# Two chained feed-forward layers behind windowed attention: the first batch's value rows loaded for all heads at once

## The chip, the cores and the metric

The kernel runs on one core of a Trainium2 chip. The metric is device time in microseconds (us) of one execution; the median of three executions of the kernel before is 607.07 us (607.02 to 609.26).

## The reference

Attention over 2 batches, 8 heads, 768 positions and 64 columns a head, then two feed-forward layers over the 1536 tokens. Each position sees the 31 keys within 15 places of its own, and 24 block summaries: the maximum of the keys and the mean of the values over blocks of 32.

```python
k_sum = k.reshape(B, H, nb, block, D).max(axis=3)
v_sum = v.reshape(B, H, nb, block, D).mean(axis=3)
scores_l = scale * q @ k.T            # kept where |i - j| < 16, else -1e9
scores_s = scale * q @ k_sum.T + log(block)
a = softmax(concat(scores_l, scores_s))
x = a @ concat(v, v_sum)              # 1536 x 512 after the heads are joined
x = (silu(x @ w_gate) * (x @ w_val)) @ w_out     # d_ff 1536
h = x @ w_in2
out = (h * tanh(softplus(h))) @ w_out2           # d_ff 2048
```

## The kernel before

**Work.** Attention goes in 24 units: batch `b`, third of the sequence `tb` (256 positions, four query tiles of 64), pair of heads `p` (units 0 to 3 are `b` 0, `tb` 0). A unit has scores (L468, `scores`), a softmax (DVE L504, L534 to L544, ACT L521), a transposition (L558) and the product with the values (L573, `values`), whose result is kept as a high and a low part, `xh` and `xl`, of reduced-precision products. The first feed-forward layer is cut into 42 items (chunk `c` of the hidden columns by token group `g`); `hidden` (L822) makes gate and value, `out_half` (L873) and `out_products` (L921) multiply by `w_out`. Later items go through `block_unit` (L1179), which saves products by sums and differences of quarters. The second layer is items 42 to 89. Feed-forward products are run as three products of high and low parts.

**Weights.** They come as 64-bit words, 512 KB to a load, through `words32` (loads `t0`, `t1`, ...): one of `NRAW` = 3 buffers `raw`, an ACT operation (L725), two or three on DVE (L732, L741, L752), then a copy (ACT, L279) and a difference (DVE, L293) give the high and low part in `wsl`. The first are `t0` (gate, chunk 0), `t1` (value), `t2` (out), `t3` to `t5` for chunk 1 and `t6` to `t8` for chunk 2. A load into `raw` can start when the words that lay there have been read.

**First batch.** `do_k` loads the transposed keys of a pair (`k0` to `k3`, into `pacc`), takes block maxima (DVE, L321) and copies all twelve overlapping key windows of 96 to `kext` on GpSimd (POOL in the profile), though units 0 to 3 read the loaded keys directly. `means_first` loads the 768 value rows as six tiles of 128 (`m0` to `m5`, 256 KB each) into scratch buffers, makes the block means of all heads in PSUM bank 0 with six fp32 products (L346; each is two instructions in the trace), and four copies, on ACT and DVE in turn (L279, L285), spread them into the value buffer `vext`. Apart from this each unit loads its own value rows (`load_v`, loads `w0`, `w1`, ...): windows of 96 rows for four query tiles by the 128 columns of its pair, 192 KB in pieces of 512 bytes. One `vext` serves all thirds and both batches.

**Order.** All operations are first collected with their dependencies and a latest time, worked back from wanted times. `Program.order` then plays them through with a model of costs and writes one fixed order for each engine and for the DMA queue of SyncE (SP in the profile). Where TensorE has nothing in that model, it puts in products on a constant tile `warm` (L266), which nobody reads. The first loads have a list of their own, `FIRST_LOADS`. Before the first operation of TensorE it puts `FILL_FIRST` = 4 of the L266 products.

Of the kernel before, what the change touches and what calls it, by code (L numbers as in the profile page):

```python
# [17 lines left out]
P = 128  # L18
# [4 lines left out]
TQ = 64  # L23
# [3 lines left out]
CCOLS = 3 * KC + P + KC + NB - P // BLOCK  # L27
# [29 lines left out]

JOIN, PAIRED = 6, 12
# [6 lines left out]
VX = ("ACT", "DVE", "ACT", "DVE")  # L65
# [3 lines left out]
def constants():  # L69
# [9 lines left out]
    out[np.arange(P), 3 * KC + P + KC - P // BLOCK + np.arange(P) // BLOCK] = 1.0 / BLOCK  # L79
# [18 lines left out]
class Program:  # L98
# [3 lines left out]
    def __init__(self):  # L102
        self.ops = []

        self.fill, self.fill_to = None, 0
        self.last_write = {}
        self.readers = {}

    def add(self, eng, cost, fn, r=(), w=(), want=None, rel=0.0):
# [15 lines left out]
        self.ops.append(dict(eng=eng, cost=cost, fn=fn, deps=sorted(deps), want=want, rel=rel))  # L125

    def order(self):
# [6 lines left out]
        dma_latency, hop = 3200.0, 250.0  # L134
        own = dict(PE=0.0, ACT=120.0, DVE=120.0, POOL=120.0, SP=0.0)
        late = [0.0] * len(ops)
        for n in range(len(ops) - 1, -1, -1):
            o = ops[n]
            t = min((late[s] for s in after[n]), default=1e9) - o["cost"] - hop
            if o["eng"] == "SP":  # L140
                t -= dma_latency
            late[n] = t if o["want"] is None else min(t, o["want"])
        left = [len(o["deps"]) for o in ops]
        ready = [o["rel"] for o in ops]
        free = dict.fromkeys(own, 0.0)
        dma_free = 1000.0
        waiting = {e: [n for n, o in enumerate(ops) if o["eng"] == e and not left[n]] for e in own}
        done = []
        while any(waiting.values()):
            best = None  # L150
            for e, c in waiting.items():
                if c:
                    t = max(free[e], min(ready[n] for n in c))
                    if e == "SP":
                        t = max(t, dma_free - 1500.0)
# [6 lines left out]
            if e == "PE" and self.fill:  # L162
                gap = t - free["PE"]
                done += [self.fill] * (FILL_FIRST if not free["PE"] else max(0, int(FILL * gap / 430.0)))
                if n == self.fill_to:
                    self.fill = None
            done.append(o["fn"])
            if e == "SP":
                free[e] = t + 450.0
                dma_free = max(dma_free, t) + o["cost"]  # L170
                end = dma_free + dma_latency
            else:
                free[e] = end = t + o["cost"]
            for s in after[n]:
# [4 lines left out]
        return done  # L179
# [10 lines left out]
def c_pool(n):  # L190
    return 100 + 2.35 * n
# [7 lines left out]
def tile_kernel(  # L199
# [25 lines left out]
    mean = cst[:, 3 * KC + P :]  # L225
    xh = many(NGRP, [P, KD, GRP], F32R, "xh")
# [1085 lines left out]
```

## Time and profile before

| | us |
|---|---|
| median of 3 runs | 607.07 |
| the profiled execution, its own time | 605.46 |
| its span, first to last instruction | 603.5 |
| TensorE busy in the span | 594.7 (99%) |
| VectorE busy | 443.8 (74%) |
| ScalarE busy | 332.3 (55%) |
| GpSimd busy | 25.0 (4%) |

The profiled execution lies 1.96 us outside its span and 1.61 us under the median. PE is TensorE, PEld its weight load, DVE VectorE, ACT ScalarE, POOL GpSimd, SPq the queue that issues DMAs. The L266 products count as busy time, so a busy TensorE isn't always one that does needed work. The mean granted clock of TensorE was 0.999 of full speed.

### The profile page before, as it was taken

What the parts mean: (1) busy time and instruction counts of PE and PEld (TensorE: products, weight loads), DVE (VectorE), ACT (ScalarE), POOL (GpSimd) and SP (SyncE); (2) the same over time, 40 slices, a digit from 0 to 9 for tenths busy, and PEclk for the clock granted to TensorE, in tenths of its full rate; (3) what the DMA queues carried; (4) which work ended last, traced back from release to release, by engine and by line L of the source; (5) the groups of instructions that cost most, each with busy time, mean ns of one, the idle gap of its engine ahead of it and who ended that gap; (6) DMA issues with size and microseconds to landing.
All of it is one profiled execution on the core that took longest, in us unless ns stands there. A gap on an engine that the chain in (4) does not pass through costs nothing.

```text
span 603.5 us, 10209 instructions
## 1 busy us (share of the span) xinstructions
PE 594.7 (99%) x3858; PEld 507.2 (84%) x3858; DVE 443.8 (74%) x1005; ACT 332.3 (55%) x764; POOL 25.0 (4%) x37
## 2 busy tenths in 40 slices
PE   8999999999999999999999999999999999999997
PEld 6688899988988889988889778988888889988875
DVE  6898689687498958858948999996574476972333
ACT  4787689655464635634525666766553465643230
POOL 3213220000000000000000000000000000000000
PEclk9999999999999999999999999999999999999999
DMA  9988566004100321302401301332130040300103
GB/s 321 303 240 220 128 197 201 29 6 153 52 1 0 141 70 45 133 33 71 141 0 33 108 2 35 105 140 84 56 107 34 1 139 1 106 0 1 70 1 139
DMA packets 34768, 55.02 MB, mean 91 GB/s; under 512 B 8712, under 2 KB 23176, under 8 KB 34720
## 3 DMA queue, kind: packets, MB, share of 16 engines
q1 hardware_dynamic: 34720, 54.38, 28.4%
q8 instruction: 30, 0.49, 0.3%
q14 instruction: 18, 0.15, 0.1%
HBM read 50.98 MB, written 3.15 MB: 90 GB/s over the span
## 4 chain that ended last, share of the span: by engine, by line
PE 93%; DVE 3%; DMA 2%; ACT 1%; issue 0%; SPq 0%; DVEq 0%
PE bank L1179 38%; PE bank L921 34%; PE bank L822 11%; PE bank L873 3%; PE bank L468 2%; PE bank L573 2%; PE bank L558 2%; DMA raw<-in_w_gate_dram 1%; DVE pacc L952 1%; PE bank L346 1%; DMA att<-in_qt_dram 1%; DVE pacc L293 1%; PE bank L266 0%; DVE xl L1079 0%; PE bank L382 0%
## 5 line engine op out<-in xcount | busy, mean ns | idle before, releaser
L1179 PE MATMUL bank<-xh,wsl 128*128 128x256 f32 (+1 forms) x512 | 142.5, 336 | 0.0
L921 PE MATMUL bank<-wsl,gt 128*128 128x512 f32 x576 | 139.1, 390 | 0.2 <-DVE pacc L952 0.2
L921 PEld LDWEIGHTS bank<-wsl,gt 128*128 128x128 f32 x576 | 106.0, 188 | 20.8 <-ACT gt L279 0.6
L1179 PEld LDWEIGHTS bank<-xh,wsl 128*128 128x128 f32 x512 | 92.0, 189 | 11.2
L293 DVE TENSOR_TENSOR tmps<-tmps,bank 128x256 f32<-128x256 f32 (+1 forms) x93 | 51.3, 551 | 66.9 <-PE bank L1179 56.5
L921 PE MATMUL bank<-gt,wsl 128*128 128x512 f32 x360 | 92.3, 392 | 1.0 <-DVE pacc L952 0.6
L1179 PE MATMUL bank<-att_late,wsl 128*128 128x512 f32 (+1 forms) x352 | 86.8, 370 | 0.0
L1179 PE MATMUL bank<-xl,wsl 128*128 128x256 f32 (+1 forms) x256 | 85.9, 336 | 0.0
L279 ACT ACTIVATE wsl<-cva 128x512 fp32r<-128x512 f32 (+1 forms) x100 | 59.1, 594 | 41.7 <-DVE cva L752 10.1
L921 PEld LDWEIGHTS bank<-gt,wsl 128*128 128x128 f32 x360 | 65.7, 188 | 14.9 <-DVE pacc L952 2.0
L822 PE MATMUL bank<-xh,wsl 128*128 128x256 f32 (+1 forms) x288 | 77.9, 328 | 0.3 <-DVE tmps L1131 0.3
L1179 PEld LDWEIGHTS bank<-att_late,wsl 128*128 128x128 f32 x352 | 64.8, 188 | 12.1 <-ACT tmps L279 0.2
L293 DVE TENSOR_TENSOR wsl<-cva,wsl 128x512 fp32r<-128x512 f32 (+1 forms) x100 | 63.8, 644 | 11.4 <-ACT wsl L279 9.9
L279 ACT ACTIVATE tmps<-bank 128x512 f32<-128x512 f32 (+1 forms) x80 | 39.1, 491 | 56.4 <-PE bank L1179 49.8
L293 DVE TENSOR_TENSOR gt<-tmps,gt 128x512 fp32r<-128x512 f32 (+1 forms) x77 | 49.6, 644 | 25.7 <-PE bank L921 13.9
L279 ACT ACTIVATE gt<-tmps 128x512 fp32r<-128x512 f32 (+1 forms) x76 | 44.9, 591 | 29.7 <-PE bank L921 21.8
L1201 ACT ACTIVATE tmps<-tmps 128x512 f32<-128x512 f32 (+1 forms) x66 | 34.5, 522 | 48.3 <-DVE tmps L293 48.1
L822 PEld LDWEIGHTS bank<-xh,wsl 128*128 128x128 f32 x288 | 51.6, 189 | 6.8 <-issue 1.8
L1179 PEld LDWEIGHTS bank<-xl,wsl 128*128 128x128 f32 x256 | 48.4, 189 | 6.3
L741 DVE SCALAR_TENSOR_TENSOR cva<-cvs,cva 128x512 uint32<-128x512 uint32 x68 | 46.7, 691 | 1.2
L725 ACT ACTIVATE cvs<-raw 128x512 f32<-128x512 f32 x68 | 45.0, 667 | 3.5 <-DMA raw<-in_w_val_dram 1.7
L822 PE MATMUL bank<-xl,wsl 128*128 128x256 f32 (+1 forms) x144 | 45.8, 318 | 0.0
(104 smaller groups left out, 721.1 us busy)
## 6 DMA issues: line engine op xcount, KB each, us to landing
raw<-in_w_out_dram SPq DMA_DIRECT2D x28, 512.0 KB, 3.7
raw<-in_w_in_dram SPq DMA_DIRECT2D x16, 512.0 KB, 3.6
raw<-in_w_gate_dram SPq DMA_DIRECT2D x12, 512.0 KB, 3.5
raw<-in_w_val_dram SPq DMA_DIRECT2D x12, 512.0 KB
att<-in_vt_dram SPq DMA_DIRECT2D x24, 192.0 KB, 5.4
att<-in_qt_dram SPq DMA_DIRECT2D x24, 128.0 KB, 4.5
out_dram<-pacc SPq DMA_DIRECT2D x8, 256.0 KB, 2.1
pacc<-in_kt_dram SPq DMA_DIRECT2D x4, 400.0 KB, 5.0
```

Source lines behind the costliest of these rows:

```text
L279: cost, fn = c_act(n, psum), lambda: nc.scalar.activation(out=dst, in_=src, func=AF.Copy, scale=scale)
L293: op(eng, c_dve(n), lambda: nc.vector.tensor_tensor(out=dst, in0=a, in1=b, op=alu), r=r, w=w)
L468: nc.tensor.matmul(parts_[2 * j + n // 2][q, cols], qb[d, n, :], moving, start=True, stop=True)
L558: nc.tensor.transpose(ps[0:KC, n * P : (n + 1) * P], s[:, n * KC : (n + 1) * KC], ident)
L573: nc.tensor.matmul(ps[d, n * TQ : (n + 1) * TQ], ve[:, n, d], pt[:, at : at + TQ], start=True, stop=True)
L725: lambda: nc.scalar.activation(out=f32(q), in_=f32(high), scale=2.0**-112, **signed),
L741: lambda: nc.vector.scalar_tensor_tensor(out=a, in0=q, scalar=3, in1=a, op0=ALU.logical_shift_left, op1=ALU.bitwise_or),
L822: nc.tensor.matmul(ps, a, x, start=(kk == 0 and m == 0), stop=(kk == KD - 1 and m == 2))
L873: nc.tensor.matmul(bank[bk][:, col : col + HALF], w[:, a, mm], gg[:, x, 0:sz], start=(n in starts and both == 1 and q == 0 and m % 2 == 0) ...
L921: nc.tensor.matmul(bank[m], lhs, rhs, start=(n in starts and both == 1 and q == 0), stop=(n in ends and both == 0),)
L1179: nc.tensor.matmul(banks[b][:, 0:wide], w, v()[:, kk, :], start=(start and kk == 0 and m == 0), stop=(kk == 1 and m == 2), skip_group_chec ...
L1201: op("ACT", c_act(wide), lambda: nc.scalar.activation(out=y, in_=src, func=func), r=r, w=[*k, *free])
```

## The change

- **Value rows of batch 0.** `first_rows(tb, half)` loads two windows of 96 rows by all 512 columns at once (384 KB in pieces of 2 KB), two such loads for each third. The thirds have a buffer each: `vext` for `tb` 0 and two new ones, `vmore`, which lie where `xh[2]` and `xl[2]` lie later. The twelve loads `w0` to `w11` go. Batch 1 still loads by unit, into `vext`.
- **Means of batch 0.** Eight of the twelve 64-row tiles are read from the windows just loaded (`m0` to `m3` are now the windows of `tb` 0 and 1); only the last third is loaded as two 128-row tiles (`m4`, `m5`). There are ten products in place of six, with 32 columns of weights in place of 120. All four copies to `vext` are on ACT. Two DMAs `e1` and `e2` copy the means from the first buffer to the other two.
- **Keys of batch 0.** `copy_window` copies only the windows of thirds 1 and 2, four tiles at a time, the last third when its units come.
- **Buffers for words.** The loads `t3` and `t4` go to `pacc[0]` (where `k0` and `k1` lay), so five loads have a place before one has to wait.
- **Planner.** Another model of costs (DMA, GpSimd, a port shared by GpSimd and VectorE, at most eight loads in flight), another `FIRST_LOADS`, the first fill from the modelled time, and `SHIFT`, which moves the latest time of named groups of operations.

```diff
+SHIFT = {
+    name: 1e3 * float(us)
+    for name, us in (
+        entry.split(":")
+        for entry in (
+            "blocks35:-0.7 blocks36:-1.1 blocks41:-1.1 blocks43:-0.6 blocks49:2.8 d12:3.7 d22:8.9 item1:-1.1 "
+            "item6:-19.1 item10:-10.7 item40:-10.3 item41:-3.3 item42:-1.7 m0:-1 m1:-0.5 out1:-2.9 out2:1.6 "
+            "out5:1.6 out7:-2.1 out8:5.7 out12:8.1 out35:-2 out41:-0.7 out42:13.4 out45:-4.6 out46:7 out48:5.6 "
+            "q1:-0.2 q6:-3.8 s8:-1 t2:2.4 t3:2 t6:-0.9 t16:2.3 t18:-6.7 words6:-2.5 words39:-9.1 words40:-5.6 "
+            "words47:-11.6 "
...
+VRATE, EARLY_RAW, NWIN = 350.0, 5, 8
...
-FIRST_LOADS = "k0 q0 k1 c0 q1 k2 c1 q2 k3 q3 t0 t1 m0 m1 m2 m3 m4 m5 w0 w1 w2 w3 t2".split()
-
-FILL_FIRST, FILL = 4, 1.2
+FIRST_LOADS = "k0 q0 c0 k1 q1 c1 m0 m1 k2 q2 k3 q3 m2 m3 t0 m4 m5 t1 t2".split()
+
+FILL = 1.2
...
+                    done += [self.fill] * max(0, int((t - 1300.0) / 630.0 if not free else FILL * (t - free) / 430.0))
...
                     if e == "SP":
-                        t = max(t, dma_free - 1500.0)
+                        t = max(t, landed[-8] + 150.0)
...
+                if o["port"]:
+                    t = max(t, port["DVE" if e == "POOL" else "POOL"])
+                    port[e] = t + o["cost"]
...
-def c_pool(n):
-    return 100 + 2.35 * n
+def c_pool(n, runs=True):
+    return 170 + (0.85 if runs else 2.1) * n
...
+    vmore = [sb.tile([P, NPAIR * 512], F32, name=f"vmore{x}", tag=f"x{x}2") for x in "hl"]
...
+    def copy_window(p, tb):
+
+        kr, t0 = kraw[p], 4 * tb
+        win = bass.AP(kr.tensor, kr.offset + t0 * TQ, [kr.ap[0], [TQ, 4], [1, WIN]])
+        copy(kext[p][:, t0 : t0 + 4, 0:WIN], win, 4 * WIN, False, kkeys[p], [("kext", p, tb)], eng="POOL")
+        copy_sums(0, p, t0, t0 + 4, [("kext", p, tb)])
+
+    def first_rows(tb, half):
+
+        src = vt[0, (4 * tb + 2 * half) * TQ :, :]
+        win = bass.AP(src.tensor, src.offset, [[DM, WIN], [TQ * DM, 2], [1, DM]])
+        keys = [("vx", tb, p, half) for p in range(NPAIR)]
+        dst = vrows[tb][0:WIN, 2 * half : 2 * half + 2, :]
+        dma(dst, win, 2 * WIN * 2048, w=keys, name=f"m{2 * tb + half}" if 4 * tb < NWIN else f"w{4 * tb + half}", rate=VRATE)
...
-        bufs = [(tmp[i], ("tmp", i)) for i in (5, 6, 7, 4, 8, 9)]
-        for t, (buf, key) in enumerate(bufs):
-            dma(buf, vt[0, WINDOW + t * P : WINDOW + (t + 1) * P, :], P * 2048, w=[key], name=f"m{t}")
-            at = NB - P // BLOCK - t * (P // BLOCK)
+        spare = [(tmp[i], ("tmp", i)) for i in (5, 6, 7, 4, 8, 9)]
+        made = [(TQ, t) for t in range(NWIN)] + [(P, t) for t in range(NWIN // 2, S // P)]
+        for n, (rows, t) in enumerate(made):
+            at, k = NB - (t + 1) * (rows // BLOCK), WIN if rows == TQ else P
+            if rows == P:
+                src, key = spare[n - NWIN]
+                dma(src, vt[0, WINDOW + t * P : WINDOW + (t + 1) * P, :], P * 2048, w=[key], name=f"m{t}")
+                keys, lhs = [key], mean2[:, at : at + 32]
+            else:
+                tb, half = t // 4, t % 4 // 2
+                if t % 2 == 0:
+                    first_rows(tb, half)
+                keys, src = [("vx", tb, p, half) for p in range(NPAIR)], vrows[tb][0:WIN, t % 4, :]
+                lhs = mean[0:WIN, at : at + 32]
...
-                [("vexts", p)],
-                eng=VX[p],
+                [("vexts", 0, p)],
             )
-
+        for tb in (1, 2):
+            dma(
+                vrows[tb][WIN:KC],
+                vrows[0][WIN:KC],
+                240e3,
+                r=[("vexts", 0, p) for p in range(NPAIR)],
+                w=[("vexts", tb, p) for p in range(NPAIR)],
+                name=f"e{tb}",
+            )
...
+        rw, kr = raw[k % NRAW], [("raw", k % NRAW)]
+        if k < EARLY_RAW:
+            n = k % (NRAW + 2)
+            rw, kr = (raw[n], [("raw", n)]) if n < NRAW else early_raw[n - NRAW]
```

## Rows read from the trace of the kernel before

**Rows 1.** The page, busy time of each engine: us, share of span, instructions.
```profile
PE 594.7 (99%) x3858; PEld 507.2 (84%) x3858; DVE 443.8 (74%) x1005; ACT 332.3 (55%) x764; POOL 25.0 (4%) x37
```

**Rows 2.** Windows of line L266 (warm products) alone: busy us of PE, PEld.
```profile
24.45:35.93 11.48, 3.94 (x16) 2.81 (x16) 1.00 1.09 299
1.00:24.45 23.45, 8.10 (x22) 4.70 (x22) 1.00 1.02 332
```

**Rows 3.** Windows of TensorE alone (all lines): busy us, granted clock, DMA share, GB/s.
```profile
24.45:35.93 11.48, 11.17 (x124) 1.00 1.09 299
```

**Rows 4.** The chain that ended last, 14 to 36 us: start, us, what.
```profile
14.83 2.58 PE bank L346 x6
...
20.45 0.60 ACT att L279
...
21.08 0.71 DVE att L285
...
25.69 0.56 DVE cva L732
...
26.30 7.18 DMA raw<-in_w_gate_dram
...
35.93 0.39 PE bank L822
```

**Rows 5.** Timeline of the DMA queue (SP): start, us, engine, line, what, count.
```profile
11.54 3.72 SPq L274 DMA_DIRECT2D att<-in_vt_dram  x4
...
22.13 1.98 SPq L274 DMA_DIRECT2D att<-in_vt_dram  x3
...
26.30 0.35 SPq L274 DMA_DIRECT2D raw<-in_w_gate_dram  x1
```

**Rows 6.** Windows of 2 us: PE, PEld, DVE, ACT, POOL; clock, DMA share, GB/s.
```profile
12.00:14.00 2.00, 2.00 (x39) 1.64 (x38) 2.00 (x13) 1.67 (x6) 0.00 (x0) 1.00 1.04 392
...
16.00:18.00 2.00, 2.00 (x9) 1.07 (x8) 1.90 (x7) 1.61 (x6) 0.00 (x0) 1.00 1.20 228
18.00:20.00 2.00, 2.00 (x6) 0.87 (x5) 1.77 (x3) 1.11 (x2) 0.00 (x0) 1.00 1.17 266
```

**Rows 7.** Timeline of TensorE, 338 to 351 us.
```profile
337.78 3.33 PE L921 MATMUL bank<-gt,wsl 128*128 128x512 f32 x14
341.44 3.69 PE L921 MATMUL bank<-gt,wsl 128*128 128x512 f32 x14 [0.33 <-ACT gt L279]
...
346.32 1.98 PE L921 MATMUL bank<-gt,wsl 128*128 128x512 f32 x8
348.62 1.43 PE L921 MATMUL bank<-gt,wsl 128*128 128x512 f32 x5 [0.33 <-DVE pacc L952]
350.36 1.42 PE L921 MATMUL bank<-gt,wsl 128*128 128x512 f32 x5 [0.30 <-DVE pacc L952]
```

**Rows 8.** The chain that ended last, an undisturbed stretch of L921.
```profile
475.09 9.52 PE bank L921 x42
```

**Rows 9.** Windows, 340 to 352 us: the same columns as in rows 6.
```profile
340.00:352.00 12.00, 11.04 (x45) 7.84 (x45) 11.98 (x15) 9.04 (x12) 0.00 (x0) 1.00 0.00 0
```

**Rows 10.** Windows of 10 us: the same columns as in rows 6.
```profile
10.00:20.00 10.00, 9.42 (x78) 5.79 (x75) 9.66 (x33) 7.23 (x27) 1.06 (x1) 1.00 1.10 335
...
30.00:40.00 10.00, 9.69 (x118) 8.37 (x116) 9.62 (x35) 7.92 (x26) 2.08 (x2) 1.00 1.03 306
```

**Rows 11.** Timeline of POOL and DVE from 9.9 to 13 us.
```profile
9.92 1.15 POOL L282 COPY att<-pacc 128x1152 f32<-128x1152 f32 x1 [0.33 <-DMA pacc<-in_kt_dram]
...
9.99 1.58 DVE L544 TENSOR_TENSOR att_tmp<-att_tmp,st 128x480 f32<-128x480 f32 x1
...
12.89 0.65 DVE L544 TENSOR_TENSOR att_tmp<-att_tmp,st 128x480 f32<-128x480 f32 x1
```

**Rows 12.** Timeline of TensorE, 0 to 2 us and 14 to 15 us.
```profile
1.10 3.78 PE L266 MATMUL bank<-warm 128*128 128x256 f32 x8 [1.10 <-POOL warm L265]
...
14.67 2.74 PE L346 MATMUL bank<-tmps,cst 128*120 128x512 f32 x6
```

More of the change, by code (lines that the diff above doesn't have):

```diff
@@ L103, in __init__, with add @@
         self.ops = []
-        self.fill, self.fill_to = None, 0
+        self.fill, self.fill_to, self.group = None, 0, None
         self.last_write = {}
         self.readers = {}
-    def add(self, eng, cost, fn, r=(), w=(), want=None, rel=0.0):
+    def add(self, eng, cost, fn, r=(), w=(), want=None, rel=0.0, group=None):
         n = len(self.ops)
@@ L124, in add @@
         deps.discard(n)
-        self.ops.append(dict(eng=eng, cost=cost, fn=fn, deps=sorted(deps), want=want, rel=rel))
+        free = cost == RECIP or any(key[0] in ("bank", "ksm") for key in (*r, *w))
+        port = eng == "POOL" or (eng == "DVE" and not free)
+        self.ops.append(dict(eng=eng, cost=cost, fn=fn, deps=sorted(deps), want=want, rel=rel, port=port, group=group or self.group))
     def order(self):
@@ L161, in order @@
             o = ops[n]
[L162 to L167, printed above, removed]
             if e == "SP":
                 free[e] = t + 450.0
-                dma_free = max(dma_free, t) + o["cost"]
-                end = dma_free + dma_latency
-            else:
+                dma_free = max(dma_free, t + 900.0) + o["cost"] * 1.08
+                end = dma_free + 1650.0
+                landed.append(end)
+            else:
+                if o["port"]:
+                    t = max(t, port["DVE" if e == "POOL" else "POOL"])
+                    port[e] = t + o["cost"]
                 free[e] = end = t + o["cost"]
+            seq.append((e, t, end, n))
             for s in after[n]:
@@ L314, in do_k @@
             win = bass.AP(src.tensor, src.offset, [[SP, P], [TQ, NTILE], [1, WIN]])
-            dma(ke[:, :, 0:WIN], win, P * NTILE * WIN * 4, w=[key], rate=200.0)
+            dma(ke[:, :, 0:WIN], win, P * NTILE * WIN * 4, w=[key, *(("kext", p, tb) for tb in range(3))], rate=200.0)
             blocks = ke[:, :, WINDOW : WINDOW + TQ].rearrange("p t (n r) -> p t n r", r=BLOCK)
@@ L437, in load_v @@
         win = bass.AP(src.tensor, src.offset, [[DM, WIN], [TQ * DM, 4], [1, P]])
-        dma(vext[p][0:WIN, :, :], win, WIN * 2048, w=[("vext", p)], name=f"w{i}", rate=240.0)
+        dma(vext[0][p][0:WIN, :, :], win, WIN * 2048, w=[("vx", 0, p, n) for n in range(2)], name=f"w{i}", rate=240.0)
     def half(i):
@@ L539, in softmax @@
         )
[L540 removed]
+        op("DVE", RECIP, lambda: nc.vector.reciprocal(out=t[:, 2, :], in_=t[:, 2, :]), w=[kt_])
         op(
@@ L599, in kv @@
             do_k(b, p)
+        if b == 0 and tb == 1:
+            copy_window(p, 2)
         loads(i)
@@ L609, in kv, with late_x, alloc @@
             value_rows(i)
-    stage = dict(s=lambda i: (kv(i), scores(i)), t=transposes, v=values)
+    def late_x():
+        def alloc():
+            for x, name in ((xh, "xh2"), (xl, "xl2")):
+                x[2] = sb.tile([P, KD, GRP], F32R, name=name, tag=name)
+        keys = [(k, tb, p, *more) for tb in (1, 2) for p in range(NPAIR) for k, *more in (("vx", 0), ("vx", 1), ("vexts",))]
+        op("DVE", 10, alloc, w=[*keys, *((x, hf, p) for x in ("xh", "xl") for hf in (4, 5) for p in range(NPAIR))])
+    stage = dict(s=lambda i: (kv(i), scores(i)), t=transposes, v=values, x=lambda i: late_x())
     steps = "s0 s1 s2 t0 s3 t1 v0 t2 v1".split()
```

157 lines of the change are left out of this document (101 added, 56 removed).

## The prediction

> **What bounds the kernel now.** I began with the page's busy line: TensorE is busy 99% of the span [rows 1], so a gain must either take products off it or turn busy time that does no needed work into work. The L266 products are such time: they multiply a constant tile that nobody reads. So I asked the windows for L266 alone. It is in the trace only before 36 us, 8.10 us of it up to 24.45 and 3.94 us from there to 35.93 [rows 2]. From 24.45 us, where the first feed-forward product starts, to 35.93 TensorE is busy 11.17 of 11.48 us [rows 3]. With the 0.31 us of idle time, 0.31 + 3.94 = 4.25 us of this stretch are lost; after it no L266 is left, and the rest of the work, some 567 us, follows almost without a pause. The reader is to see that whatever brings the end of this stretch forward, with the same work done by then, moves the whole rest forward.
>
> What ends it is told by the chain of waits [rows 4]: products of the means (two stretches of six, 2.58 us each), the copies of the means in turn on ACT and DVE, then a DVE operation on loaded words (L732), which frees the buffer in which `t6` is to land; the load is issued at 26.30 [rows 5] and takes 7.18 us [rows 4]; its words are converted, and 35.93 follows. So two things delay `t6`: it waits for a buffer, and then it shares a full DMA. The DMA share is 1.00 or more [rows 3, 6]. What it moves in that time varies: 392 GB/s at 12 to 14 us, but 228 and 266 in the two slices from 16 us [rows 6], while the four loads `w0` to `w3`, issued from 11.54 to 15.26 [rows 5], are under way.
>
> A second place is at 340 us, where the layers meet: three pauses of TensorE [rows 7]. At the rate of an undisturbed stretch, 9.52 / 42 = 0.227 us a product [rows 8], the 14, 8 and 5 products before these pauses would take 3.18, 1.82 and 1.13 us; start to start they take 3.66, 2.30 and 1.74. That is 1.6 us lost. DVE is busy 11.98 of these 12 us [rows 9], and DVE additions end two of the pauses.
>
> **The change part by part.** *Value rows.* Up to `t6` seven unit loads of 192 KB (four and three, [rows 5]; the size from 96 x 4 x 128 numbers) and six of 256 KB come in: 2880 KB. Afterwards: four of 384, two of 256, and the copies `e1` and `e2` of 192 each: 2432. So 448 KB less, at 392 GB/s [rows 6] 1.2 us. Then the pace: from 16 to 20 us 2 x (228 + 266) = 988 thousand bytes moved [rows 6]; at 392 GB/s that is 2.5 us, so the four loads in 512-byte pieces cost 1.5 us beyond their bytes, and seven would cost 2.6. Together 3.8 us, if all of it is the pieces. `t6` would land near 33.5 - 3.8 = 29.7. Of a gain of 0 to 3.8 I keep both ends.
>
> The Trainium skill, "DMA: Bandwidth & Descriptors" (Specifications), puts the least transfer at line rate at 512 B: the removed pieces would already run at full rate, and only the 1.2 us of bytes would be won. The slow slices speak against it, but they also hold other loads, so I carry this as a rival.
>
> *Buffers.* With five places `t6` needs only `t0` to have been read, and no longer waits for the DVE operation at 25.69 [rows 4]. Now 7.18 us lie between issue and landing, so an earlier issue alone can't win more than the queue lets through; it is what makes the DMA gain usable, and I add nothing for it.
>
> *What else could hold that stretch.* DVE is busy 9.66 and 9.62 of ten us on either side of it, ACT 7.23 and 7.92 [rows 10]. DVE loses two copies of means of 0.71 us [rows 4], 1.4 in all; ACT gains two of 0.60, 1.2, and has 2.8 us free in the ten before. GpSimd copies two thirds of the key windows, in eight pieces in place of four. A DVE multiplication that takes 0.65 us took 1.58 beside such a copy [rows 11]; there is 0 to 0.9 us in that. So DVE gives back 1.4 to 2.3 us, plus its 0.34 and 0.38 us of idle time [rows 10]: 1.8 to 3.0. DMA allows 3.8, TensorE's lost time 4.25, DVE up to 3.0. I take **3.0**, because conversions that start earlier also spread into idle time before 10 us; the lower bound is 0, the upper 4.25.
>
> *Means.* Each of the now six products costs two instructions, 2.58 / 6 x 2 = 0.86 us [rows 4]; ten cost 8.6, so 3.4 us more on TensorE. I cost this at nothing, and the cover must be named. Of 8.10 us of L266 before 24.45 [rows 2], 3.78 run before the first scores [rows 12] and cover nothing; 4.3 remain. The windows `m0` and `m1` now stand seventh and eighth in the list, not thirteenth, and the sizes ahead of them (about 1.4 MB against 3.5) put them, in proportion to the bytes, at 7 to 9 us; the first means product of today starts at 14.67 [rows 12]. So 3.4 of 4.3 us fit. If the cover fails, up to 3.4 us are late: the copies, then `xh`, then the first feed-forward product. The copies on ACT alone take 4 x 0.60 = 2.4 us against 2 x (0.60 + 0.71) = 2.6 in turn. Nothing, within 0.2. `e1` and `e2` wait in SP's queue for those copies; behind them stand `t3` and later loads, whose fellows already in flight cover some us. Units 4 to 7 now need `e1`, some 10 us after it is issued. Nothing.
>
> *Keys.* GpSimd is 4% busy [rows 1]; the copies for the last third must free `pacc[0]` before `t3` is loaded, which is some 10 us after the keys land. Nothing.
>
> *First fill.* The new rule may put in more than four L266 products before the first scores; they run at about 0.47 us an instruction there [rows 12], two instructions a product. First scores may come 1 us late, but the mask constants are now third in the list. Nothing, plus or minus 0.5.
>
> *Batch 1.* Its first loads need units 0 to 3 to be done, not 8 to 11; TensorE has no pause there. Nothing.
>
> *Order by the new model.* Of the named shifts about half concern items 35 to 49 and their words, which is where 1.6 us are lost [rows 7]. Taking word conversions out of a stretch in which DVE is full [rows 9] can win all of it; that the order merely moves the pauses is as possible. Between 0 and 1.6 I take **1.0**. Elsewhere TensorE has no slack to win; a new order could open pauses, which is what the upper end of the range is for.
>
> Sum: 3.0 + 1.0 = 4.0 us. From the profiled execution's own 605.46 that gives 601.5; that one lies 1.61 under the median of the runs, so the median goes from 607.07 to **603.1**. What this measurement can tell from no change is 0.5%, 3.0 us: below 604.0 is faster, above 610.1 slower.
>
> **The rivals.** *Only bytes or only engines.* The slow slices were not the pieces, or DVE and ACT hold the stretch whatever lands. For it: DVE above 96% on both sides [rows 10]. Against: the chain shows a 7.18 us load, not DVE [rows 4]. The first gives 1.2 + 1.0: 604.9; the second 0 to 1.0: 606.1 to 607.1. Under the Trainium skill's rule above it would be the first.
>
> *Everything fills.* No L266 from the first feed-forward product on, and all three pauses go: 4.25 + 1.6 = 5.9, so 601.2; with an earlier first product by 1.0 to 1.5 as well, 599.7 to 600.2. For it: the DMA gain and the buffers together reach back to `t3`. Against: DVE's upper bound of 3.0.
>
> *The means take TensorE's time (slower).* If `m0` still lands near 14.5 us, since several loads in flight share the queue, all ten products run one after another: 14.7 + 8.6 plus the transposition between them is 23.8 against 20.4 now [rows 4], 3.4 us late, and everything after it. With no gain elsewhere 610.5, with the pauses gone 608.9. It decides once the last means product ends after about 23.5; up to 21 it is hidden. Against: three quarters of the DMA traffic that stands ahead of `m0` today goes behind it.
>
> **How the numbers follow.** The forecast (a gain of 2.5 to 5.5 us) has 0.50, 0.04 of it between 604.0 and 604.6; everything fills 0.14; only bytes or engines 0.24; means late 0.12. Faster: 0.14 + 0.46 of the first = 0.60. Slower: the means case without any gain, and pauses opened by the new order, 0.10. Same: 0.30. The range goes from 599.5, the best case, to 608.0, which takes in the hidden case and part of the late one; 0.07 lies below and 0.12 above. The forecast's own range is 601.6 to 604.6.
>
> **What would show it.** Right: a first means product before 10 us and the last by 21; DMA slices of 350 GB/s and more from 10 to 30 us; `t6` landed by 30; few L266 after the first feed-forward product, and none after 32; fewer than three pauses at 340. Wrong: L266 still in the trace at 34 us, DVE without a gap from 10 to 32 with words waiting for it, a pause before the values of unit 4 for `e1`, or a first feed-forward product after 26 us.

## The result, and the profile after

The changed kernel takes 612.08 us (median of 19 executions, 609.03 to 618.31) beside 606.30 us for the kernel before (19 executions, 605.64 to 609.26): a ratio of **1.0087, 95% interval 1.0068 to 1.0105**. It is slower by 0.9%, where I forecast 603.1 us and gave slower a chance of one in ten. Ratios leave out executions in a slower state of the chip, here the one of 618.31 us and in `e13` one of 617.75, so this one is not the quotient of the two medians. The profiled execution took 610.01 us, with a span of 608.2. The first lines of its page, which answer to [rows 1]:

```profile
span 608.2 us, 10207 instructions
PE 597.3 (98%) x3860; PEld 506.2 (83%) x3860; DVE 442.3 (73%) x1003; ACT 333.9 (55%) x766; POOL 23.0 (4%) x45
```

The loss has two parts. In nine of the 19 executions the mean granted clock was 0.998 or more; they took 609.03 to 612.28 us, median 610.26, so 3.96 us more than before. In the other ten it was 0.982 to 0.997, and they took 611.84 to 618.31. The median of all stands 1.82 us above that of the nine.

TensorE's timeline in the changed kernel shows where the 4 us of the first part go. Line 310 is now the warm product, 411 the means, 544 the scores, 635 the transposition, 651 the values, 930 the first feed-forward product, 1029 and 1288 the later ones.

```profile
1.10 5.71 PE L310 MATMUL bank<-warm 128*128 128x256 f32 x14 [1.10 <-POOL warm L309]
6.74 0.49 PE L544 MATMUL bank<-pacc,att 64*64 64x96 f32 x8
...
9.99 2.73 PE L411 MATMUL bank<-att,cst 96*32 96x512 f32 x6
...
16.55 1.04 PE L411 MATMUL bank<-vmoreh,cst 96*32 96x512 f32 x2 [0.60 <-DMA vmoreh<-in_vt_dram]
...
18.60 2.76 PE L411 MATMUL bank<-vmoreh,cst 96*32 96x512 f32 x6
...
22.74 1.05 PE L411 MATMUL bank<-tmps,cst 128*32 128x512 f32 x2
...
25.29 1.15 PE L651 MATMUL bank<-att_tmp,att 120*64 120x64 f32 x32
...
29.42 0.39 PE L930 MATMUL bank<-xh,wsl 128*128 128x256 f32 x1
...
41.56 0.65 PE L635 MATMUL bank<-cst,att_tmp 128*120 128x128 f32 x4 [1.73 <-DVE att_tmp L621]
...
344.17 3.22 PE L1029 MATMUL bank<-gt,wsl 128*128 128x512 f32 x12 [0.33 <-ACT gt L323]
...
351.62 1.43 PE L1029 MATMUL bank<-gt,wsl 128*128 128x512 f32 x5 [0.61 <-DVE pacc L1060]
353.36 1.43 PE L1029 MATMUL bank<-gt,wsl 128*128 128x512 f32 x5 [0.30 <-DVE pacc L1060]
...
366.18 0.50 PE L1288 MATMUL bank<-xh,wsl 128*128 128x512 f32 x1 [0.97 <-ACT kx L1310]
```

The first means products run at 9.99 us, as early as I said. But those of the second third can't start before 16.55, when their window rows (`m2`) have landed, and the last ends at 23.79 (22.74 + 1.05) where it ended at 20.43 before [rows 4]. The first feed-forward product starts at 29.42, five microseconds after that of before [rows 2]. Then comes a pause that was not there: 1.73 us at 41.56. The three pauses near 350 us are all still there, at 0.33, 0.61 and 0.30 us against 0.33, 0.33 and 0.30 [rows 7], and a fourth of 0.97 us has joined them.

The chain of the changed kernel for the same stretch, to be held against [rows 4]:

```profile
7.50 9.00 DMA vmoreh<-in_vt_dram
...
16.55 1.04 PE bank L411 x2
...
18.67 3.55 PE bank L411 x8
...
23.82 2.04 ACT att L323 x4
...
29.70 0.46 ACT wsl L323
30.16 10.32 DMA raw<-in_w_out_dram
...
40.51 0.43 DVE cva L838
40.94 0.58 DVE att_tmp L621
```

Two transfers carry it: `m2`, 9.00 us from issue to landing, and the words `t5`, 10.32 us. Between them stands ScalarE: the four copies of the means start at 23.82, when the last means product is done, and the words of `t2`, in whose buffer `t5` is to land, are read behind them, at 28.04 (ScalarE's timeline, L831), where the kernel before reads them at 23.92 (L725).

```profile
28.04 0.72 ACT L831 ACTIVATE cvs<-raw 128x512 f32<-128x512 f32 x1
```

```profile
23.92 0.71 ACT L725 ACTIVATE cvs<-raw 128x512 f32<-128x512 f32 x1
```

The DMA queue of the changed kernel (columns as in [rows 5]) shows that `t6` and `t7` did go out earlier, at 23.11 and 24.40 us. It was `t5`, which has none of the five early places, that became the late one: issued at 30.16, where the queue of the kernel before has it at 24.90, ahead of the `t6` of [rows 5] (its line has a fence of its own).

```profile
23.11 0.33 SPq L318 DMA_DIRECT2D raw<-in_w_gate_dram  x1
24.40 0.33 SPq L318 DMA_DIRECT2D raw<-in_w_val_dram  x1
24.78 0.92 SPq L318 DMA_DIRECT2D vmorel<-in_vt_dram  x2
...
26.78 0.90 SPq L318 DMA_DIRECT2D vmoreh<-att  x1
...
30.16 0.33 SPq L318 DMA_DIRECT2D raw<-in_w_out_dram  x1
```

```profile
24.90 0.35 SPq L274 DMA_DIRECT2D raw<-in_w_out_dram  x1
```

VectorE has its instructions in one fixed order, and its timeline shows what stands behind those words: the softmax multiplication (L621), for which TensorE waits.

```profile
40.51 0.43 DVE L838 TENSOR_SCALAR cva<-raw 128x512 uint32<-128x512 uint32 x1 [1.69 <-DMA raw<-in_w_out_dram]
40.85 0.65 DVE L621 TENSOR_TENSOR att_tmp<-att_tmp,st 128x480 f32<-128x480 f32 x1
```

The windows of the changed kernel, and one of the kernel before in a fence of its own, columns as in [rows 6]:

```profile
12.00:14.00 2.00, 2.00 (x8) 0.55 (x6) 1.57 (x4) 0.63 (x2) 1.43 (x4) 1.00 1.06 330
14.00:16.00 2.00, 1.95 (x37) 1.46 (x36) 1.80 (x7) 0.02 (x1) 1.64 (x4) 1.00 1.06 231
16.00:18.00 2.00, 1.46 (x18) 0.62 (x22) 0.32 (x4) 2.00 (x9) 0.00 (x0) 1.00 1.04 285
```

```profile
14.00:16.00 2.00, 2.00 (x10) 1.20 (x9) 2.00 (x12) 2.00 (x11) 0.00 (x0) 1.00 1.06 389
```

And the windows of L310 alone, to be held against [rows 2] (PE, PEld, clock, DMA share, GB/s):

```profile
1.00:24.45 23.45, 6.96 (x19) 5.20 (x20) 1.00 1.00 300
24.45:29.42 4.97, 2.04 (x8) 1.13 (x7) 1.00 1.05 385
29.42:41.56 12.14, 1.78 (x6) 0.93 (x6) 1.00 1.08 217
```

The DMA is as full as before (shares of 1.00 to 1.08), but the slow slices have not gone. They have moved: 231 GB/s from 14 to 16 us, where the kernel before has 389, and 217 GB/s from 29.42 to 41.56, after the window rows of the last third (24.78) and the copies `e1` (26.78) and `e2` (32.38) were issued. Warm products fall from 12.04 us [rows 2] to 6.96 + 2.04 + 1.78 = 10.78, by 1.26. But the first fill grew from 3.78 us [rows 12] to 5.71. Behind the first scores they fall from 12.04 - 3.78 = 8.26 to 10.78 - 5.71 = 5.07, so 3.19 of the 3.44 us of four added means products did take the place of warm products.

At the new pause of 0.97 us, ScalarE loads a table just ahead of the activation for which TensorE waits (ScalarE's timeline):

```profile
363.20 1.28 ACT L1310 ACT_TABLE_LOAD   x1
...
365.56 0.58 ACT L1310 ACTIVATE kx<-bank 128x512 f32<-128x512 f32 x1
```

### The profile page after: what moved, and what is told of

The parts are those of the page before. It is cut to its first block, busy times and chain, and to the rows that moved or that the text cites. A ratio compares the mean times of both kernels' runs of the same rounds, so it can differ in the third digit from the quotient of the medians.

```text
span 608.2 us, 10207 instructions
## 1 busy us (share of the span) xinstructions
PE 597.3 (98%) x3860; PEld 506.2 (83%) x3860; DVE 442.3 (73%) x1003; ACT 333.9 (55%) x766; POOL 23.0 (4%) x45
## 4 chain that ended last, share of the span: by engine, by line
PE 89%; DMA 5%; DVE 3%; ACT 2%; issue 0%; SPq 0%; DVEq 0%; ACTq 0%
PE bank L1288 37%; PE bank L1029 32%; PE bank L930 10%; PE bank L981 3%; PE bank L651 2%; DMA raw<-in_w_out_dram 2%; PE bank L544 2%; PE bank L635 2%; DMA vmoreh<-in_vt_dram 1%; DVE pacc L1060 1%; PE bank L411 1%; DMA att<-in_qt_dram 1%; DMA raw<-in_w_in_dram 1%; DVE pacc L337 1%; DVE xl L1188 0%
## 5 line engine op out<-in xcount | busy, mean ns | idle before, releaser
L1288 PE MATMUL bank<-xh,wsl 128*128 128x256 f32 (+1 forms) x512 | 141.5, 336 | 1.0 <-ACT kx L1310 1.0
L1288 PEld LDWEIGHTS bank<-xh,wsl 128*128 128x128 f32 x512 | 91.5, 189 | 12.4 <-ACT kx L1310 1.4
L930 PE MATMUL bank<-xh,wsl 128*128 128x256 f32 (+1 forms) x288 | 75.6, 326 | 0.0
L831 ACT ACTIVATE cvs<-raw 128x512 f32<-128x512 f32 x66 | 43.8, 669 | 13.4 <-DVE cva L847 4.5
```

Of the source, the lines that this page charges most:

```text
L831: lambda: nc.scalar.activation(out=f32(q), in_=f32(high), scale=2.0**-112, **signed),
L930: nc.tensor.matmul(ps, a, x, start=(kk == 0 and m == 0), stop=(kk == KD - 1 and m == 2))
L1288: nc.tensor.matmul(banks[b][:, 0:wide], w, v()[:, kk, :], start=(start and kk == 0 and m == 0), stop=(kk == 1 and m == 2), skip_group_chec ...
```

## The experiments

All ratios are against the kernel before, run beside each version: its median is 606.28 us beside `e1` to `e4`, 606.55 beside `e5` to `e8`, 607.34 beside `e9` to `e12` and 606.44 beside `e13` to `e16`. So times of two versions are compared by how far each lies above its own kernel before; for the changed kernel at a granted clock of 0.998 or more that is the 3.96 us above. Diffs are against the changed kernel unless it says "before"; `...` marks what is left out.

**Are the four added products the cost?** `e1_six` makes the means from six 128-row tiles again; the windows are still loaded once for all heads, so 1 MB more is loaded than in the changed kernel.

```diff
-VRATE, EARLY_RAW, NWIN = 350.0, 5, 8
+VRATE, EARLY_RAW, NWIN = 350.0, 5, 0
...
-FIRST_LOADS = "k0 q0 c0 k1 q1 c1 m0 m1 k2 q2 k3 q3 m2 m3 t0 m4 m5 t1 t2".split()
+FIRST_LOADS = "k0 q0 c0 k1 q1 c1 k2 q2 k3 q3 m0 m1 m2 t0 m3 m4 m5 t1 w0 w1 t2".split()
```

> The means are made from six tiles of 128 rows as before; all value windows are still loaded once for all heads, afterwards. Theory products (the ten products of the means stand on TensorE's path, four more than before, 3.4 us): the last means product ends 2.5 to 3.5 us earlier than 23.8 and the ratio to the kernel before falls from 1.009 to 1.003 to 1.005. Theory transfers (the loads of 96-row windows are slow and hold everything): a megabyte more is loaded, 2.6 us at 390 GB/s, so no gain, ratio 1.009 to 1.014. Theory order (the new order by itself costs the time): ratio stays at 1.009.

Measured: 609.61 us, 1.0051 [1.0036, 1.0067]; granted clock 0.998 or more in all six executions. Its last means product ends at 19.20 us and its first feed-forward product starts at 25.51, both some 4 us ahead of the changed kernel's. Yet its executions take 608.74 to 610.80 us, a median 3.33 us above the kernel before, where the changed kernel at that clock is 3.96 above: of the 4 us hardly one is left. A late last means product is therefore not by itself what decides. What was saved was lost again, as it seems in loads; its chain up to 46 us has these two, the first of value rows:

```profile
12.32 11.05 DMA att<-in_vt_dram
...
25.54 9.26 DMA raw<-in_w_gate_dram
```

`e9_sixof` does not issue four of the ten products and keeps the order of everything else.

```diff
+SKIP = (1, 3, 5, 7)
...
-                lambda n=n, lhs=lhs, src=src: nc.tensor.matmul(
+                lambda n=n, lhs=lhs, src=src: n in SKIP
+                or nc.tensor.matmul(
```

> The changed kernel in its own order, but four of the ten products of the means aren't issued, so that the block means of four 64-row tiles are wrong; everything else is issued as before. This takes 3.4 us of TensorE's work away at its place. Theory products: the last means product ends 2.5 to 3.4 us earlier and the ratio falls from 1.009 to 1.003 to 1.005. Theory transfers (the windows and the late words of w_out decide): the later loads don't move, the pause near 40 us eats what was won, ratio 1.007 to 1.009.

Measured: 611.09 us, 1.0066 [1.0045, 1.0087]. Not conclusive: in its profile the granted clock is 0.50 from 12.40 to 26.00 us, and five of its six executions have a mean of 0.993 or less. The sixth, at 1.0, took 609.51, 2.2 us above the kernel before.

**The first fill, the copies, more fill.** `e2_fill4` puts in four warm products before the first scores, as before.

```diff
-... int((t - 1300.0) / 630.0 if not free else FILL * (t - free) / 430.0))
+... int(4 if not free else FILL * (t - free) / 430.0))
```

> Four warm products before the first scores in place of seven. Theory products: TensorE works through its list from the first scores to the last means product almost without a gap, so the first scores at 4.9 instead of 6.7 us bring the last means product forward by 1 to 1.9 us, ratio 1.006 to 1.007. Theory transfers: the second value window lands at 16.5 us whatever TensorE does, so 0 to 0.5 us, ratio 1.008 to 1.009.

Measured: 612.45 us, 1.0104 [1.0072, 1.0137]: no gain, though five of its six executions have a mean granted clock below 0.998. Its profile tells why none was to be had: the first scores start at 4.81 us and not at 6.74, but the last means product ends at 23.74 (23.79 in the changed kernel), since `m2` is waited for until 16.50 all the same. Its windows show something else (columns as in [rows 6]):

```profile
39.80:42.50 2.70, 0.43 (x6) 0.42 (x5) 1.46 (x3) 1.46 (x4) 0.28 (x1) 1.00 1.16 217
42.60:45.90 3.30, 3.30 (x29) 3.08 (x27) 3.30 (x16) 3.28 (x12) 0.00 (x0) 0.50 0.95 229
```

TensorE is busy 0.43 of 2.70 us, in the pause for `t5` (2.27 us here); then its granted clock is 0.50, the lower level of 1.2 GHz, for 3.3 us.

`e15_fill2` doubles the fill between items (`FILL = 1.2` becomes `2.4`).

> The changed kernel with twice as many warm products in the modelled gaps (not before the first scores); nothing else. Theory clock (a part of the median's loss is the granted clock of TensorE, which falls to half in some executions after pauses in the first 50 us): runs lie closer together, median at or under that of the changed kernel, ratio 1.006 to 1.009, lowest run not lower than 609. Theory fills cost: the added products stand before needed ones, 1 to 3 us more in every run, ratio 1.009 to 1.014.

Measured: 612.45 us, 1.0103 [1.0087, 1.0119], executions of 612.17 to 612.92, all with a granted clock of 0.998 or more. The clock no longer falls, but the time is 6.0 us above the kernel before, against 3.96 for the changed kernel at that clock. In its profile TensorE waits near 11 us without a fall of the clock behind it:

```profile
11.29 2.73 PE L411 MATMUL bank<-att,cst 96*32 96x512 f32 x6 [0.90 <-DMA cst<-in_consts_dram]
```

`e3_poolmeans` replaces the two transfers `e1` and `e2` by eight GpSimd copies.

```diff
-            dma(
-                vrows[tb][WIN:KC],
-                vrows[0][WIN:KC],
...
+            for p in range(NPAIR):
+                copy(
+                    vext[tb][p][WIN:KC, :, :],
+                    vext[0][p][WIN:KC, :, :],
...
+                    eng="POOL",
```

> The means go to the other two buffers by eight GpSimd copies in place of the two DMAs. Theory transfers: the load of the words of w_out that was issued at 30.16 and took 10.3 us takes under 8, the pause of TensorE of 1.73 us at 40 us goes: 1.5 to 2.5 us less, ratio 1.005 to 1.0065. Theory products: that pause is filled by later work anyway, ratio 1.008 to 1.009. Theory order: no statement but a change of less than 1 us.

Measured: 615.15 us, 1.0143 [1.0124, 1.0162]. Worse; the order changed with the costs, and the granted clock is 0.50 from 12.3 to 15.7 us, behind a wait for the constants. It clears nothing of the transfers.

```profile
11.84 4.43 PE L411 MATMUL bank<-att,cst 96*32 96x512 f32 x6 [1.29 <-DMA cst<-in_consts_dram]
```

**The order.** `e4_noshift` is the changed kernel without its table of shifts. `e5_newplan` is the kernel before under the new planner and its costs, without shifts. `e6_oldplan` is the changed data path under the planner of before, with the changed list of first loads.

```diff
# e4_noshift: the table of shifts
-    "blocks35:-0.7 blocks36:-1.1 ... words47:-11.6 "
+    ""
# e5_newplan, against before: the planner's model and costs, of which
-    t = max(t, dma_free - 1500.0)
+    t = max(t, landed[-8] + 150.0)
...
# e6_oldplan: the same line, back
-    t = max(t, landed[-8] + 150.0)
+    t = max(t, dma_free - 1500.0)
...
```

> All named shifts of latest times are taken out; everything else is the changed kernel. Theory order: the three pauses near 343 to 353 us and the new one of 0.97 us at 365 (together 2.8 us of lost time) change; if the shifts made them, ratio 1.004 to 1.006. Theories products and transfers: the first 45 us keep their loss, ratio within 0.002 of 1.009; as the shifts might also help, 1.008 to 1.013.

> The kernel before, with the new planner and its costs, without any named shift; loads, means, key copies and buffers stay as before. Theory order (the new planner's order costs time, the shifts win most of it back): slower by 0.8 to 2%, 611 to 618. Theory data path (means products and window loads make the loss; the order is neutral): within 0.4% of the kernel before.

> The changed kernel's loads, means, key copies and buffers under the old planner with its costs and its first fill of four; no shift; the new list of first loads. Theory order: 603 to 606, the data path's gain shows, ratio 0.995 to 1.000. Theory data path: the ten products and the slow windows cost 2.5 to 4 us as in the changed kernel, ratio 1.004 to 1.008, and the first feed-forward product still starts after 27 us.

Measured: e4 618.65 us, 1.0201 [1.0184, 1.0218]; e5 615.18 us, 1.0140 [1.0122, 1.0158]; e6 617.58 us, 1.0181 [1.0150, 1.0211]. TensorE's waits in e5 show where a replanned kernel loses part of its 8.6 us with nothing else changed (us in total, times, longest):

```profile
PE bank L1200 <- ACT tmps L299: 2.8, 4, 1.2
PE bank L579 <- ACT att_tmp L299: 1.8, 1, 1.8
```

The planner alone, with its costs and its first fill, costs 1.4%. The new data path alone, under the planner of before, costs 1.8%; its executions all have a mean granted clock below 0.998, so a part of this is the clock. Both without shifts cost 2.0%, so the two do not add. The shifts win back 618.65 - 612.08 = 6.6 us. The first of these waits is in e4 too (2.7 us in four) and not in the changed kernel, so the shifts mend the new order there; no run has them under the planner of before.

**The transfers.** `e8_loads` leaves out all work but loads of value rows, six shapes one after another, 192 to 384 KB a load, several in flight at a time, and stores of the tiles of the first shape.

```diff
+    (rows128, lambda i: src(i, [[DM, P], [1, 512]])),
+    (win96, lambda i: src(i, [[DM, 96], [TQ * DM, 2], [1, 512]])),
+    (piece96, lambda i: src(i, [[DM, 96], [TQ * DM, 4], [1, 128]])),
+    (rows96, lambda i: src(i, [[DM, 96], [1, 512]])),
+    (piece128, lambda i: src(i, [[DM, P], [TQ * DM, 4], [1, 128]])),
+    (rows64, lambda i: src(i, [[DM, 64], [TQ * DM, 2], [1, 512]])),
```

> Only loads of value rows, in six stages of 1.5 to 4 MB, each stage after the one before has landed: tiles of 128 rows, two windows of 96 rows with 2 KB pieces, four windows of 96 rows with 512-byte pieces, 96 rows without overlap, 128 rows in 512-byte pieces, two windows of 64 rows; the attention and both layers are left out. Theory pieces (what the prediction took: 512-byte pieces are slow, 2 KB pieces are not): 380 to 400 GB/s in the first, second, fourth and sixth stage, 200 to 270 in the third and fifth. Theory partitions (a load to 96 partitions is slow whatever its pieces): 380 to 400 in the first and fifth, 220 to 290 in the second, third and fourth.

Measured, one window for each of these six shapes, in this order (DVE, POOL, clock, DMA share, GB/s):

```profile
8.00:16.00 8.00, 1.70 (x11) 0.00 (x0) 1.00 1.04 392
20.00:30.00 10.00, 0.82 (x6) 0.00 (x0) 1.00 1.06 246
38.00:46.00 8.00, 1.55 (x10) 0.00 (x0) 1.00 1.22 244
50.00:58.00 8.00, 1.71 (x12) 0.00 (x0) 1.00 1.02 300
66.00:76.00 10.00, 1.39 (x9) 0.00 (x0) 1.00 1.11 290
82.00:90.00 8.00, 0.93 (x6) 0.00 (x0) 1.00 1.06 211
```

Rows of 2 KB into 128 partitions move at 392 GB/s. The new window loads, two overlapping windows of 96 rows in 2 KB pieces, move at 246, no faster than the removed ones in 512-byte pieces at 244. The pieces are not what made them slow. (In the second stage three stores of 256 KB, issued from 20.47 us, run beside the loads; VectorE's timeline has a load landed at 23.93, 25.67, 27.46 and 29.22, so the windows alone came at 384 KB in 1.76 us, 223 GB/s.) What did is in part the number of partitions: without overlap 128, 96 and 64 of them take 392, 300 and 211 GB/s, 3.1 to 3.3 for each. Windows that overlap are slower still, 246 and 244 against 300 at 96 partitions. In the fifth shape windows overlap and pieces are small, so its 290 against 392 can't be put down to one of the two. The theory of the pieces has the second and the sixth shape wrong, that of the partitions the fifth, and the fourth by 10 GB/s.

`e10_narrow` loads 320 of the 512 columns of each window with the order fixed, 37.5% fewer window bytes; the other columns are zero, so it leaves out their values.

```diff
+NCOL = 320
...
-    win = bass.AP(src.tensor, src.offset, [[DM, WIN], [TQ * DM, 2], [1, DM]])
+    win = bass.AP(src.tensor, src.offset, [[DM, WIN], [TQ * DM, 2], [1, NCOL]])
...
```

> The changed kernel in its own order; the window loads of value rows bring only 320 of the 512 columns (the rest is zero, so the values of those columns are left out), 62% of the bytes, which at 240 GB/s take as long as all would at 385. Theory transfers: the second window of third 1 lands near 13 instead of 16.5 us, the words of w_out land before 37, the pause near 40 us goes, ratio 1.002 to 1.005. Theory products: TensorE is full of products from 17 to 24 us anyway, ratio 1.007 to 1.009.

Measured: 608.20 us, 1.0011 [0.9999, 1.0023]; 12 executions of 607.49 to 608.79, all with a granted clock of 0.998 or more. Its windows, columns as above in the changed kernel:

```profile
14.00:16.00 2.00, 2.00 (x37) 1.32 (x36) 1.56 (x3) 0.37 (x1) 1.85 (x5) 1.00 1.01 362
16.00:18.00 2.00, 2.00 (x30) 0.99 (x32) 0.75 (x8) 1.58 (x7) 0.00 (x0) 1.00 1.06 402
```

362 and 402 GB/s stand where the changed kernel has 231 and 285, `m2` is not waited for, and there is no pause at 41 us. The ratio falls from 1.0087 to 1.0011, and its interval takes in no loss at all. At equal clock, 608.20 is 0.86 us above the 607.34 beside it, 3.1 us less than the 3.96 of the changed kernel; the rest is that the clock no longer falls. TensorE's timeline shows where:

```profile
342.44 3.23 PE L1030 MATMUL bank<-gt,wsl 128*128 128x512 f32 x12 [0.33 <-ACT gt L324]
```

This pause is at 341.44 us in the kernel before [rows 7] and at 344.17 in the changed kernel, and in all three 1284 instructions of TensorE are left from there on. So e10 is 1.73 us ahead of the changed kernel there, the length of the pause at 41.56, and only 1.00 behind the kernel before, although it has all ten means products, the last ending at 23.54, and its first feed-forward product still starts at 29.18.

**The late words.** `e11_t5early` puts `t5` into the second key buffer and issues it after `t4`; `e13_t5free` puts it into a free scratch tile at the same place.

```diff
# e11_t5early, in the loads; in the order, t5 moves up behind t4
+    if k == 5:
+        rw = pacc[1][:, 0:2, :].rearrange("p m f -> p (m f)").bitcast(U32)
...
# e13_t5free, likewise
+    if k == 5:
+        rw = tmps[:, 3:5, :].rearrange("p m f -> p (m f)").bitcast(U32)
...
```

> The changed kernel in its own order, except that the sixth load of words (t5, w_out of chunk 1) goes into the second key buffer and is issued right after t4, near 22 us, not at 30.16 when the buffer of t2 is read. Theory buffer (the 1.7 us pause at 40 us is the wait of VectorE's queue for t5): the pause goes, 1.5 to 2.5 us less and a steadier clock, ratio 1.004 to 1.006. Theory products: the pause only held what the next loads hold a little later, ratio 1.007 to 1.009.

> The changed kernel in its own order, except that the sixth load of words (t5) lands in scratch tiles that are free until later, and is issued right after t4. In e11 it took the place of a load that others waited for. Theory buffer: VectorE's queue no longer waits for t5 at 40 us, the pause of 1.7 us goes, ratio 1.003 to 1.006. Theory transfers (the queue is full of slow window loads, so what comes earlier pushes other loads back): the pause moves to another load, ratio 1.007 to 1.010.

Measured: e11 618.56 us, 1.0180 [1.0154, 1.0207]. It tells nothing of `t5`: the buffer held up the value tiles of batch 1 (a wait of 4.3 us of TensorE), and their loads overwrote part of the words, so its output is that of other words. e13 610.17 us, 1.0067 [1.0044, 1.0090]. The pause at 41.56 is gone; the longest wait left in TensorE's timeline there is this one:

```profile
39.86 0.39 PE L934 MATMUL bank<-xh,wsl 128*128 128x256 f32 x1 [0.37 <-DVE tmps L1244]
```

Its three executions at a granted clock of 0.998 or more took 608.51, 609.53 and 609.93 us; the middle one is 3.1 us above the kernel before, 0.9 less than the changed kernel's 3.96, and three executions are few. In its profile the clock was 0.50 from 10.90 to 21.10, with the mask constants landing late on the chain (7.24 us), and that execution took 613.09.

**The small parts alone, all against before.** `e7_early` gives the first five words places of their own; `e12_mfirst` also loads the means tiles ahead of the words; `e14_keys` copies only the key tiles that are read; `e16_early_keys` joins the first and the third.

```diff
# e7_early
+EARLY_RAW = 5
+    if k < EARLY_RAW:
+        n = k % (NRAW + 2)
+        rw, kr = (raw[n], [("raw", n)]) if n < NRAW else early_raw[n - NRAW]
...
# e12_mfirst, on top
-FIRST_LOADS = "k0 q0 k1 c0 q1 k2 c1 q2 k3 q3 t0 t1 m0 m1 m2 m3 m4 m5 w0 w1 w2 w3 t2".split()
+FIRST_LOADS = "k0 q0 k1 c0 q1 k2 c1 q2 k3 q3 m0 m1 m2 t0 m3 m4 m5 t1 w0 w1 w2 w3 t2".split()
# e14_keys
-    copy(ke[:, :, 0:WIN], win, NTILE * WIN, False, kb, [key], eng="POOL")
...
+    copy(ke[:, 4:, 0:WIN], win, (NTILE - 4) * WIN, False, kb, [key], eng="POOL")
...
```

> The kernel before with five places for the first words (t3 and t4 into the key buffer), nothing else. If the wait of t6 for a buffer was on the path: t6 lands 1 to 3 us before 33.5 and the time falls by 1 to 3 us, ratio 0.995 to 0.998. If the full queue decides alone: t3 to t6 only trade places with other loads, ratio 0.999 to 1.002.

> The kernel before with five places for the first words, and the six tiles for the means ahead of the words in the list of first loads; no other change. If the end of the means sets the first feed-forward product there too: the first means product at 12 to 13 us instead of 14.67, the first feed-forward product 1 to 2 us earlier, ratio 0.994 to 0.998. If the words then come too late for the first items, or the new order opens stalls: 0.999 to 1.005.

> The kernel before, with the key copies of batch 0 cut to the eight tiles that are read; nothing else is changed, the old planner makes the order. If GpSimd's copies hold VectorE on the path: ratio 0.996 to 0.999. If nothing waits for them: 0.999 to 1.002; a larger change either way would be the work of the new order alone.

> The kernel before with five places for the first words and the key copies of read tiles only: the two parts of the change that leave loads and means alone. If both are independent of the slow windows: ratio 0.995 to 0.999, a kernel faster than both. If the order answers to any small change with a stall: 0.999 to 1.006.

Measured: e7 605.60 us, **0.9983 [0.9971, 0.9995]**; e12 607.43, 1.0002 [0.9989, 1.0014]; e14 606.61, 1.0005 [0.9995, 1.0016]; e16 606.12, 0.9993 [0.9981, 1.0005]. The early places are the only part that gains anything, 0.2%, and e7 is the only version whose interval lies below 1. e16 has the same places and 1 inside its interval, so this gain is at the edge of what these runs can tell. With the means tiles brought forward it is not to be seen (e12); the key copies are worth nothing that can be measured.

## Why the prediction was wrong

**Value rows (3.0 us taken, up to 3.8 worked out).** This is the step that failed first. I put the 228 and 266 GB/s of [rows 6] down to 512-byte pieces and took the new loads at 392 GB/s. e8 shows the shape of the windows to be what is slow: 246 GB/s with 2 KB pieces, 244 with 512 bytes. So the change did not remove slow loads: twelve of 192 KB and six of 384 KB are the same 2304 KB of window rows. What went is four tiles of 128 rows, the fast kind, and four window loads now stand in front of means products in their place. `m2` needed 9.00 us, and e10 shows that the kernel gets back nearly all of its loss when the windows are 37.5% smaller. The rule of the Trainium skill that I carried as a rival ("DMA: Bandwidth & Descriptors", Specifications: line rate from 512 B on) was nearer for these loads, since the pieces of 512 B and 2 KB are alike at 96 rows. At 128 rows e8 has 290 GB/s in 512-byte pieces against 392, but those windows also overlap, so it does not decide on the rule.

**Means (nothing taken, 3.4 us as the price if the cover fails).** The first products came at 9.99 us, one microsecond behind the 7 to 9 us that I worked out for their tiles. (By the sizes that I gave, 1.4 MB against 3.5, three fifths of the traffic ahead of `m0` went behind it, and not the three quarters of the rival's last sentence.) The cover held in amount, 3.19 us of warm products for 3.44. The second step, that the last product ends by 21 us, failed: I had asked when `m0` lands, and not when the last window does. The products of the second third could not start before 16.55, and the last ended at 23.79, the very end that the rival had for all ten in a row (23.8), though by another cause. The price was not paid in full either: e10, with all ten products and the last one at 23.54, is 1.00 us behind the kernel before where the layers meet. What the late means did was to put their copies, now all on ScalarE, 3.4 us back, and with them the reading of `t2`'s words 4.1 us. How much of the 1.00 us is the four products is not shown: in e9 the clock fell, and in e1 the loads grew.

**Buffers (nothing added).** That `t6` would no longer wait for that buffer was right; it was issued 3.2 us earlier. What I did not ask is which word comes next. `t5` has no place among the five and waits for `t2`'s words to be read, and the words of `t5` hold VectorE's queue with a softmax step behind them. e13 shows that the pause of 1.73 us goes when `t5` has a place. e7 shows that the places alone, in the kernel before, gain 0.2% at most.

**Keys, first fill, `e1` and `e2` (nothing).** Keys were right (e14). The first fill made no difference: it grew by 1.93 us, and e2 takes that back without moving the last means product. TensorE's timeline has no wait of a values product for `e1` or `e2`; what they cost the other loads is not shown, since in e3 the order and the clock changed too.

**Order (1.0 us taken).** I read shifts on items 35 to 49 as a gain on [rows 7]. The pauses there total 1.24 us against 0.96, and a new one of 0.97 follows: 1.25 us worse where I had 1.0 better. The step went wrong in its reference: the shifts act on the order of a new planner, which alone costs 1.4% (e5), and they win 6.6 us of that side back (e4).

**The clock, which had no term.** The rows show 1.00 throughout [rows 3, 6], and I had no rival in which it falls. In ten of 19 executions the mean is below 0.998. e2's profile shows one fall, from 2.4 to 1.2 GHz for 3.3 us, after TensorE had been busy 0.43 of 2.70 us. In e3, e4, e9 and e13 the fall comes between 10.9 and 12.4 us, behind waits of 1.29, 1.34, 1.12 and 0.92 us for the constants or the first window rows. But e15 and e2 wait there too, 0.90 and 1.08 us, and keep the clock, and e1 has a pause of 1.29 us at 50.04 and 0.998 or more in all six executions. So pauses go ahead of each of these falls, and no run shows which pause brings one on. No profile of the changed kernel has a fall, and why one execution has it and the next does not stays open.

Of the rivals, "the means take TensorE's time" had the right sign, and its 608.9 to 610.5 holds the 610.26 at full clock. That is luck: its rule, that the end of the last means product decides, does not hold. e10's ends at 23.54 and loses 0.9 us, and e1's ends at 19.20 and loses 3.3. What e1, e8 and e10 point to together is the time that the DMA needs for all that the first 42 us want.

The base was off as well: the three executions that I started from have a median of 607.07 us, all 19 one of 606.30. By the profiles the loss comes in this order. Where the layers meet, the changed kernel is 344.17 - 341.44 = 2.73 us behind: 1.73 is the pause for `t5`, and 1.00 is all the rest of the first 42 us. The later pauses add 1.25. That makes 3.98 of the 4.7 us by which the spans differ; some 0.7 us after the pause at 366 I could not name. This is one profile of each kernel, and executions of one kernel differ by 2 us and more. Also open is why overlapping windows are slow: e8 shows that the 96 partitions have a part (300 GB/s without overlap) and that the overlap has another, and no run tells how either comes about.

## What to carry to other kernels

Where a stretch has its DMA full, price each load by its shape and not by its bytes or its pieces alone: measure the rate of that very access pattern, since here 128 rows, 64 rows and overlapping windows of 96 differ by 392 to 211 and 246 GB/s. Ask of a step that is split over several loads when the last of them lands, and which load is next in line for a buffer when one is freed. Compare a version with the old kernel run beside it, since the latter's median alone moved by 1 us between groups here. When a change brings a new order with it, run the old work under the new order first: here that alone cost 1.4%, more than the 0.9% of the whole change.

## What the runs showed of the hardware that I had not expected

In e8, 128 plain rows load at 392 GB/s, 96 at 300 and 64 (two windows without overlap) at 211, so 3.1 to 3.3 GB/s for each partition. Two windows of 96 overlapping rows load at 246, four in 512-byte pieces at 244, and four of 128 overlapping rows in 512-byte pieces at 290. All have the 16 DMA engines shown as full (shares of 1.02 to 1.22). Pauses of TensorE early in the kernel can be followed by several microseconds at the lower clock: 3.3 us in e2 behind a pause of 2.27, 3.4 in e3 behind one of 1.29, 10.2 in e13 behind 0.92 and 13.6 in e9 behind 1.12; behind pauses of 0.90 in e15 and 1.08 in e2 there is none. In e11 one late load with other work behind it on VectorE cost TensorE 4.3 us in a single wait.
